# An RWKV-6 attention with a Gelu MLP: later tiles' second product by 20 block products

## The chip, the cores and the metric

The kernel runs on one core of a Trainium2 chip. A time is the device time of one execution in microseconds. Engines are called as in the profile: PE (TensorE's matmuls) and PEld (its weight loads), DVE (VectorE), ACT (ScalarE), POOL (GpSimd), SP (SyncE, which here only issues DMAs). Each works through its own instructions strictly in the order in which they are written.

## What is computed

An attention whose state decays by w at every token, and a two-layer MLP on its output. Batch 4, 8 heads, 768 tokens, head size 48; the attention's output is laid out as x with 3072 tokens of 384; w_in is 384 x 2048, w_out 2048 x 384. All is float32.

```python
for t in range(S):
    cur = einsum('bhd,bhe->bhde', u * k[t], v[t])
    y[t] = einsum('bhd,bhde->bhe', r[t], state + cur)
    state = w[t][..., None] * state + einsum('bhd,bhe->bhde', k[t], v[t])
x = y laid out as (3072, 384)
h = x @ w_in
g = 0.5 * h * (1 + erf(h / sqrt(2)))
out = g @ w_out
```

## The kernel before

**Tiles and stages.** The tokens are cut into eight tiles of T = 384 (NX = 8). For a tile, `attention(x, 0)` gives xT, the transposed input of the MLP, and `mlp(x)` does the MLP. Stage x runs `mlp(x - 1)` together with the end of `attention(x, 0)` and the beginning of `attention(x + 1, 0)`. Stage 0 is attention alone; a last stage, 8, is `mlp(7)` alone.

**The order is written out.** Every part is a Python generator that yields after each small step, and the string `PLAN[x]` says which generator steps next: "." is the MLP's matmuls, "s" and "f" the two attentions (s the one under way, f the following), "l" loads, "x" the eleven sums of x on DVE (`sums_of_x`, L960, tile forms_x), "g" what follows the first product, "w" the sums of the weights, "c" the conversion of the weights. So each engine's queue is fixed by these strings. What holds an instruction back is a semaphore on another engine's work, or a buffer.

**First product (h).** Tile 0 does it plainly (L1093, 128x384 matmuls). Tiles 1 to 7 compute it by 20 block products (`PRODUCTS`, `STEPS`, L1006) for each of two groups q, from sums of blocks of x and w_in. The results are gathered in g, four tiles of 128 x 4 x 384: by copies on ACT (L1025), by accumulating DMAs from POOL ("m", L1052), and by DVE adds from SBUF ("v", L1054) and from PSUM ("+" and "-", L1057). `FOLLOW` lists these merges and the Gelus on ACT (L1067) in one order for each q; a name such as 03 is half 0 of the 384 tokens (192 of them) and group 3 of the 2048 columns of h.

**Second product (out).** It works on blocks of 128 tokens. Tile 0 does its first two blocks plainly, 128x384 (L1181). Tiles 1 to 7 do blocks 0 and 1 by seven products of a 2x2x2 scheme (`product`, L1107, eight matmuls of 128x192 each). The third blocks go in pairs: an even tile (`waits`) keeps its third block apart in `alone`, does two products of it, and the following odd tile (`ends`) does five more on both. The sums of g that the scheme needs (s1, s2, s3) are made by DVE into tiles of their own (`of_g`, L998 to L1002, and L1155 to L1214), those of w_out once, in stage 2 (`w_sums`, `first_sum`). The products alternate between the two PSUM banks that `bank()` hands out in turn.

**PSUM.** Eight banks: from stage 2 on two for `bank()`, two called u0 and u1 (`bank_u`), and two pairs for the attention (`pair`). The attention's last burst of scores (`burst`, L654) uses u0 and u1 in even tiles.

**The attention's order on DVE** that matters here: while the second product of a tile runs, DVE carries the states from chunk to chunk (L792), multiplies u, r and k for the next tile (L457), and then copies two elements of each y bank (`fences`, L830). PE's last matmuls into y (L863) wait for these copies. The six buffers o_sb (`OUTS`) hold saved banks and rows of the output until their DMA has read them.

Of the kernel before, what the change touches and what calls it, by code (L numbers as in the profile page):

```python
# [39 lines left out]
    0: "l.s....llsl.lssslslss.lc.l.slslls...ssss..lcs.s.s.l.ss..ss..sccs.c.s.llpssslw..cs.ffpccxx",  # L40
    1: (
        "scs.ccs..cwsclcs.l.cclcsccssccs.ccc.cswcscccw..swsccls.cccscsc.sscww.lsc.swwcc.ccc.lwllcsl"
        ".fccwcwscc...fccfccws.f.cc.c.w.c.cccfxwcwxcw.c.xx.wcxwcw.fxw.wxx.x.w.fxf.xw.fl."
    ),
    2: (
        "wwws.w.s.wws.w..w..w.gsw..ww.ggw..s..ggwssg.w.ssw.gwgwgg.wslw.ggglww..g.w.s.w..gl..gswgg.s"
        "......wgg.gggg.gglgs.gggggwgs.gs..ssg.lsggs.sgsgwsgw..l.s....s..sssssl..l.lf.sfs.f.ff.lx.w"
        "xxxxxxx.x.xx"
    ),
    3: (  # L50
        "..s....s..s.g.l..g..gsgss....gllgs.ggsg.g..sss.gsgss.s.gs..ggs.g.s.ssg..s.ss.g.s.l.ggsgs.."
        "g.ggggggggssggslgggg.sggg.s....l.sg..sslllss...sslf.ff...xxx.xxxxxx.xx"
    ),
    4: (
        ".s..s.s.sl..s...sgg..s...gg.gg.sg.gl..sgl.ggs...ggg.s.gss.sss...sg.gg.glg...ls.g.sgg.gg.gg"
        "s.sggsgg.g.s.ggs.sg.gsls.g.gssg..sg....ss.sllss.ls..f.ssf.f.f.fx..xx.xxxxlxxfxx"
    ),
    5: (
        ".ls......gls...g.s..s.gl...ggg..gs.sg.ls.gssggsg.gssg.slssss.ls....g..sggsg..ss..ssgg.gsgs"
        "g..g..gggggsgg.ggg.sgg.g.s.sgs.g..sl.l.s.glssfsffs....lfxxxxxxxx..xxx."  # L60
    ),
    6: (
        ".s.ll....sg.s...ss...sg..gssggl.g...gg.sgg..ggss..ggss..s.ss..gs..s.sglggggs...gs.gg..g.g."
        "ggsssgsgsgsg..gg.gg.g...sgggsssg..l...l..s.slsl.s.lf.ss.ff.lff.x..xx.xxxxxfxfxx"
    ),
    7: (
        ".s..s...s...s....gg..g..gs.ggggs...ggg.ssgs.ssgg.s..g.s.gg.s.ssss..s.sgsg..gs.gs..sgg.gggg"
        ".ggggs.g..gsgsg.s.sggg..gg..s.s.sss..ss.xx..xx.x.xxxxxx"
    ),
    8: (  # L70
        "...........g...gg.gg..g.g..ggg.gg..g.g...g.g..gg.g..g...g...gg.gggggg.g.gg.ggg...gggg..g.."
        ".................."
# [50 lines left out]
    "P3", "P12 se", "P17 =cb", "P0 1a00", "P5 =db", "P1 1c03", "P7 1a10", "P8 1b12", "P15 sd+1", "P4 1a11",  # L123
    "P6", "P2 1b02", "P13", "P16 sd+2", "P9 1a13", "P11 sb-", "P10 sa", "P14", "P18", "P19",
)
FOLLOW = (
    (
        "me>00", "md1>11", "me>02", "md2>12", "g00", "mb>03", "ma>03", "+d10", "-c02", "-b13", "G01", "g11",
        "g02", "g10", "g13", "g12", "g03",
    ),  # L130
    (
        "me>00", "md1>11", "me>02", "md2>12", "g00", "vb>03", "va>03", "+d10", "-c02", "-b13", "G01", "g12", "g02",
        "g03", "g13", "g11", "g10",
    ),
# [8 lines left out]
def kernel(  # L143
# [45 lines left out]
    def bank(name="o_ps"):  # L189
        return ps.tile([128, BANK], F32, name=name, tag="mm", bufs=2)  # L190
# [13 lines left out]
    alone = bufs[0][:, ALL:ALL + NF * 128].rearrange("p (f t) -> p f t", f=NF)  # L204
    p1_alone = bufs[0][:, ALL + NF * 128:ALL + NF * 128 + DM // 2]
# [82 lines left out]
    def keep_warm(n, elsewhere=False):  # L288
        if elsewhere:
            t = pair("warm")[:, 0]  # L290
        else:
            t = ps.tile([128, BANK], F32, name="warm", tag="mm", bufs=2)
        for _ in range(n):
            nc.tensor.matmul(t, lhsT=zeros[:, 0:128], rhs=zeros, start=True, stop=True)
# [127 lines left out]
    def attention(x, unit):  # L422
# [183 lines left out]
        def quarters():  # L606
# [28 lines left out]
            for h in QUARTERS:  # L635
                m, r4, t4, s0, s1, s2 = views(h)

                def burst(first, behind, spare=False):

                    d = [bank_u(i) for i in range(2)] if spare else pair("d")  # L640
# [8 lines left out]
                    for n in range(first, behind):  # L649
                        i = n - first  # L650
                        for g in range(2):
                            for p in range(2):
                                o = d[g] if isinstance(d, list) else d[:, g]
                                nc.tensor.matmul(o[half[p], i * 3 * C // 2:(i + 1) * 3 * C // 2],  # L654
                                                 lhsT=kc[half[g], n // NI, n % NI, p],
                                                 rhs=rx[half[g], 2 * n + p], start=not spare or i == 0, stop=True,
                                                 skip_group_check=True)
# [14 lines left out]
                def copy_quarters(first, behind, d):  # L672
                    if isinstance(d, list):
                        for g in range(2):
                            copy_rows(first, behind, d[g][:, 0:(behind - first) * 3 * C // 2].rearrange("p (n x) -> p n x", n=behind - first), g)
                        return
# [14 lines left out]
                whole = last and x % 2 == 0  # L691
                cuts = (0, n_b // 3, 2 * n_b // 3, n_b) if whole else (0, 5, 10, n_b)
                parts_of = list(zip(cuts, cuts[1:]))
                ds = [burst(*parts_of[0])]
                if not whole:
                    yield
                ds.append(burst(*parts_of[1]))
                if whole:
                    ds.append(burst(*parts_of[2], spare=True))
# [3 lines left out]
                if not whole:  # L703
                    ds.append(burst(*parts_of[2]))
                    yield
# [101 lines left out]
        def inside():  # L807

            for b in range(np_):
                if split:  # L810
                    y = [ps.tile([128, BANK], F32, name="y_ps", tag="mm", bufs=2) for _ in range(2)]
                else:
                    y_ps = pair("y_ps")
                    y = [y_ps[:, c] for c in range(2)]
# [82 lines left out]
    HF, HM = NF // 2, DM // 2  # L897
    FG = 4
    sums, s3_sb = [], []

    def w_quarter(b, c, k):
        return w_out_sb[:, b * HF + k * FG:b * HF + (k + 1) * FG, c * HM:(c + 1) * HM]

    def w_sums():

        sums.extend(cv.tile([128, HF, HM], F32, name="t", tag="raw", bufs=AHEAD) for _ in range(3))
        for out_, x, y in ((0, (0, 1), (0, 0)), (1, (1, 1), (0, 1)), (0, (1, 1), 0), (2, (1, 0), 0)):
            for k in range(2):
                o = sums[out_][:, k * FG:(k + 1) * FG]
                nc.vector.tensor_sub(o, w_quarter(*x, k), sums[y][:, k * FG:(k + 1) * FG] if isinstance(y, int) else w_quarter(*y, k))  # L910
                yield

    def first_sum():
        for k in range(2):
            nc.vector.tensor_sub(w_quarter(0, 1, k), w_quarter(0, 1, k), w_quarter(0, 0, k))
            yield

# [3 lines left out]
    s12_of = {}  # L921
    forms_x = const.tile([128, 10, HT], F32, name="forms_x")
    extra = {i: s_home[:, n * 2 * WI:(n + 1) * 2 * WI].rearrange("p (q c) -> p q c", q=HK) for n, i in enumerate((0, 5))}

    def homes():

        more = [cv.tile([128, PIECE], I64, name="s", tag="raw", bufs=AHEAD).bitcast(F32) for _ in range(2)]
        s3_sb.append(more[0][:, 0:HF * 128].rearrange("p (f c) -> p f c", f=HF))
        spare = [cv.tile([128, PIECE], F32, name=name) for name in ("f", "f", "e", "e")]
        for i, name in enumerate(("s1", "s2")):  # L930
            s12_of[name] = [z[:, 0:FG * 128].rearrange("p (f c) -> p f c", f=FG) for z in spare[2 * i:2 * i + 2]]
        for z, at, i in ((more[0], HF * 128, 3), (more[1], 0, 1), (more[1], 2 * WI, 2), (more[1], 4 * WI, 6)):
            extra[i] = z[:, at:at + 2 * WI].rearrange("p (q c) -> p q c", q=HK)
        for n, i in enumerate((4, 7)):
            extra[i] = [z[:, FG * 128:] for z in spare[2 * n:2 * n + 2]]

# [33 lines left out]
    follow_of = {}  # L970

    def follow(x):
        while x in follow_of:
            if next(follow_of[x], follow_of) is follow_of:
                return
            yield

    def mlp(x):

        halves = x > 0
        waits, ends = x % 2 == 0, x % 2 == 1
        gs = {}

        def block(a, b, j):
            return gs[2 * b + j // FG][:, j % FG, a * 128:(a + 1) * 128]

        def store(row0, o_sb, c0=0):
            nc.sync.dma_start(out=out[row0:row0 + 128, c0:c0 + o_sb.shape[1]], in_=o_sb)  # L990

        def of_g(k):

            s1.append(s12_of["s1"][k])
            s2.append(s12_of["s2"][k])
            s3.append(s3_sb[0][:, k * FG:(k + 1) * FG])
            a00, a10, a11 = (gs[g][:, :, a:a + 128] for g, a in ((k, 0), (k, 128), (k + 2, 128)))
            nc.vector.tensor_add(s1[k], a10, a11)  # L998
            yield
            nc.vector.tensor_sub(s2[k], s1[k], a00)  # L1000
            yield
            nc.vector.tensor_sub(s3[k], a00, a10)  # L1002
            yield

        def multiply(o, lhsT, rhs, start=False):
            nc.tensor.matmul(o, lhsT=lhsT, rhs=rhs, start=start, stop=True, skip_group_check=True)  # L1006

        def h_forms():

            for group in range(4):  # L1010
                gs[group] = gp.tile([128, FG, T], F32, name="g")
            banks, saved = {}, {}

            def g_of(q, h):
                a, j = int(h[0]), int(h[1])
# [332 lines left out]
```

## Time and profile before

| what | before |
|---|---|
| median of 3 runs | 593.14 us (592.83 to 593.51) |
| the profiled execution | 591.54 us |
| its span, first to last instruction | 589.4 us |
| mean granted TensorE clock | 0.997 |
| DMAs that accumulate into g | 70, 192 KB each |
| stores of the output | 20 of 192 KB, 8 of 96 KB |

The profile is of one execution. A busy PE is one whose modelled matmuls cover the time. A window is a stretch of the span with each engine's busy time in it. A wait is idle time of an engine just before an instruction, put down to the instruction that released it.

### The profile page before, as it was taken

The page shows a single profiled execution, that of the slowest core. Times are in us where ns is not written, and L with a number is a line of the kernel's source. Part 1 is how long each engine was busy: PE and PEld are TensorE (multiplying, and loading weights), DVE is VectorE, ACT ScalarE, POOL GpSimd, SP SyncE. Part 2 cuts the span into 40 slices and gives each one's busy share as a digit, 9 for nine tenths or more (in the row PEclk, how much of TensorE's full clock was granted, in tenths as well). Part 3 has the DMA queues.
Part 4 walks back from the last instruction along what each step waited for, and adds up shares of the span by engine and source line. Part 5 has one row for each costly group of instructions (what it writes and reads, how often), then busy time and mean ns, then how long its engine had stood idle before and what let it go on. Part 6 is the DMA issues. An engine that isn't in the chain of part 4 may idle for free.

```text
span 589.4 us, 17720 instructions
## 1 busy us (share of the span) xinstructions
PE 561.7 (95%) x7490; PEld 504.0 (86%) x7504; DVE 462.7 (79%) x933; ACT 315.4 (54%) x724; POOL 92.6 (16%) x91
## 2 busy tenths in 40 slices
PE   5789999999999999999999999899999999999997
PEld 3566666699999988897999988898998988999997
DVE  6979979999979986888869997689859997541162
ACT  2358998257542677246652476435771467536600
POOL 3100000034000430023200321004300042005200
PEclk8999999999999999999999999999999999999999
DMA  7649662255152743356322563336533354215500
GB/s 246 206 124 372 209 229 68 68 136 74 23 130 76 146 56 51 113 145 125 42 55 78 149 116 55 82 127 97 70 60 100 86 70 54 41 46 68 68 14 33
DMA packets 70046, 60.59 MB, mean 103 GB/s; under 512 B 32848, under 2 KB 55120, under 8 KB 69968
## 3 DMA queue, kind: packets, MB, share of 16 engines
q1 hardware_dynamic: 50832, 45.62, 25.3%
q0 software_dynamic: 19040, 13.77, 17.9%
q8 instruction: 59, 0.97, 0.7%
q14 instruction: 19, 0.16, 0.1%
q10 hardware_dynamic: 96, 0.07, 0.1%
HBM read 36.24 MB, written 4.72 MB: 69 GB/s over the span
## 4 chain that ended last, share of the span: by engine, by line
PE 39%; DVE 15%; ACT 5%; issue 2%; DMA 1%; SPq 1%; DVEq 0%
PE o_ps L1107 19%; PE h_ps L1006 8%; PE u_ps L1006 5%; DVE rkw L485 3%; PE d L654 3%; DVE kx L451 2%; ACT a_sb L670 2%; DVE rkw L444 2%; DVE st L792 2%; DVE kx L457 2%; PE y_ps L863 2%; DVE forms_x L967 1%; SPq L893 1%; PE kv_ps L777 1%; DMA g<-o_sb 1%
## 5 line engine op out<-in xcount | busy, mean ns | idle before, releaser
L1052 POOL DMA_DIRECT2D g<-o_sb x70 | 84.6, 1264 | 449.5 <-ACT g L1025 413.5
L1006 PE MATMUL h_ps<-forms_x,w_in_sb 128*128 128x192 f32 x280 | 57.3, 332 | 0.0
L1025 ACT COPY g<-h_ps 128x384 f32<-128x384 f32 x84 | 40.2, 481 | 16.6 <-PE h_ps L1006 14.4
L1006 PEld LDWEIGHTS h_ps<-forms_x,w_in_sb 128*128 128x128 f32 x280 | 46.4, 190 | 2.9 <-ACT g L1025 2.1
L1025 ACT COPY o_sb<-u_ps 128x384 f32<-128x384 f32 x42 | 20.2, 481 | 44.6 <-PE u_ps L1006 44.6
L1107 PE MATMUL o_ps<-w_out_sb,g 128*128 128x192 f32 x224 | 39.5, 330 | 4.1 <-ACT g L1067 3.5
L1107 PEld LDWEIGHTS o_ps<-w_out_sb,g 128*128 128x128 f32 x224 | 36.3, 190 | 6.3 <-ACT g L1067 5.3
L670 ACT COPY a_sb<-d 32x256 f32<-32x256 f32 (+8 forms) x90 | 32.6, 363 | 7.6 <-PE d L654 4.2
L1006 PE MATMUL h_ps<-xT,w_in_sb 128*128 128x192 f32 x168 | 35.0, 331 | 1.6 <-DVE g L1057 1.1
L1067 ACT ACTIVATE g<-g 128x384 f32<-128x384 f32 x74 | 35.8, 519 | 0.8 <-DMA g<-o_sb 0.7
L1006 PE MATMUL h_ps<-forms_x,s 128*128 128x192 f32 x168 | 35.8, 336 | 0.3 <-ACT u_ps L1025 0.3
L1093 PE MATMUL h_ps<-xT,w_in_sb 128*128 128x384 f32 x96 | 33.5, 496 | 0.0
L1006 PE MATMUL u_ps<-xT,w_in_sb 128*128 128x192 f32 x168 | 32.7, 331 | 0.8 <-DVE g L1057 0.6
L792 DVE SCALAR_TENSOR_TENSOR st<-st,tot_sb,kv_ps 128x48 f32<-128x48 f32 x160 | 29.1, 256 | 5.3 <-PE kv_ps L777 5.2
L518 PEld LDWEIGHTS d<-rkw 64*64 64x64 f32 x1152 | 19.4, 137 | 14.4 <-issue 9.4
L1107 PE MATMUL o_ps<-w_out_sb,e 128*128 128x192 f32 x176 | 30.9, 328 | 0.5 <-ACT o_sb L1152 0.5
L1107 PE MATMUL o_ps<-t,g 128*128 128x192 f32 x176 | 31.1, 329 | 0.0
L1107 PE MATMUL o_ps<-w_out_sb,f 128*128 128x192 f32 x176 | 31.1, 329 | 0.0
L1107 PE MATMUL o_ps<-t,s 128*128 128x192 f32 x176 | 30.8, 327 | 0.0
L1006 PEld LDWEIGHTS h_ps<-xT,w_in_sb 128*128 128x128 f32 x168 | 28.0, 190 | 3.2 <-DVE g L1057 1.4
L1107 PE MATMUL o_ps<-t,e 128*128 128x192 f32 x176 | 30.5, 326 | 0.0
L1006 PEld LDWEIGHTS h_ps<-forms_x,s 128*128 128x128 f32 x168 | 27.6, 190 | 3.1 <-ACT u_ps L1025 2.3
(177 smaller groups left out, 1268.0 us busy)
## 6 DMA issues: line engine op xcount, KB each, us to landing
rkw<-in_rkw_dram SPq DMA_DIRECT2D x54, 256.0 KB, 3.5
g<-o_sb POOLq DMA_DIRECT2D x70, 192.0 KB, 3.6
raw<-in_w_out_dram SPq DMA_DIRECT2D x8, 768.0 KB, 5.0
v_in<-in_v_dram SPq DMA_DIRECT2D x8, 584.0 KB, 3.9
raw<-in_w_in_dram SPq DMA_DIRECT2D x5, 768.0 KB, 8.2
out_dram<-o_sb SPq DMA_DIRECT2D x20, 192.0 KB, 2.2
rkw<-kx SPq DMA_DIRECT2D x72, 48.0 KB, 2.0
rkw<-in_rkw_dram SPq DMA_DIRECT2D x6, 384.0 KB, 5.1
```

The costliest lines, as they stand in the source:

```text
L444: nc.vector.tensor_reduce(out=fine_sb[:, e, 0:n].rearrange("p a n -> p (a n)"), in_=kx[:, o:o + n * n_m].rearrange("p (m j) -> p m j", j=3 ...
L485: nc.vector.tensor_mul(z, z, by)
L518: nc.tensor.matmul(d[half[p], g, n * width:(n + 1) * width], lhsT=kc[half[g], b, i, p], rhs=right(half[g], b, i, p), start=True, stop=True)
L654: nc.tensor.matmul(o[half[p], i * 3 * C // 2:(i + 1) * 3 * C // 2], lhsT=kc[half[g], n // NI, n % NI, p], rhs=rx[half[g], 2 * n + p], star ...
L670: nc.scalar.copy(out=at[z, g, first:behind, (a + 1) * h:], in_=d[z, :, :, to] if g == slice(None) else d[z, :, to])
L792: nc.vector.scalar_tensor_tensor(out=stq[:, q, c], in0=stq[:, q, c - 1] if c else b4[:, q, NC - 1], scalar=totq[:, q, c:c + 1], in1=kvs[q ...
L1006: nc.tensor.matmul(o, lhsT=lhsT, rhs=rhs, start=start, stop=True, skip_group_check=True)
L1025: nc.scalar.copy(out=o, in_=z)
L1052: nc.gpsimd.dma_start(out=o, in_=saved[q, t], accum_op=ALU.add)
L1067: nc.scalar.activation(out=o, in_=z, func=AF.Gelu, scale=s)
L1093: nc.tensor.matmul(h_ps, lhsT=w_in_sb[:, f // FI, j, f % FI * 128:(f % FI + 1) * 128], rhs=xT[:, j, :], start=(j == 0), stop=(j == NJ - 1))
L1107: nc.tensor.matmul(o, lhsT=lhs(j), rhs=rhs(j), start=start and j == 0, stop=(j == HF - 1), skip_group_check=True)
```

## The change

- Tiles 1 to 7 compute the whole second product by 20 products of a 3x4x2 scheme: three blocks of 128 tokens, four groups of 512 columns of h, two halves of 192 output columns. Each product is four matmuls of 128x192. Pairs of tiles are no longer tied together. `alone` only gives room for sums of w_out.
- The sums of g are made in place, in g itself: 16 adds of 128 x 512 for a tile. A sum may stand only behind the product that reads the earlier content. Ten accumulators share the banks m0, m1, u0 and u1. Some are seeded by a copy of another (S), some are saved (V) and added later (M), and their parts are added to rows of the output by DVE or copied by ACT.
- Tile 0 does all three blocks plainly, the third in a loop of its own.
- In the first product, group q = 0 saves banks c, d and b by ACT ("0sc-", "0sd", "0sb-2") and merges them by accumulating DMAs; these were DVE adds from PSUM. In the last tile all such DMAs become DVE adds.
- `bank()` takes a bank's number. The attention's last burst no longer uses u0 and u1.
- Sums of w_out: 16 in place of 10 blocks, ten of them in stage 1 (stream "y").
- Merges ("v"), Gelus ("g"), sums of g ("o") and copies ("e") are streams of their own, and all of `PLAN` is new.

```diff
+MERGES = (
+    ("me>00", "md1>11", "me>02", "md2>12", "mc>02", "mb>03", "md>10", "mb2>13", "ma>03"),
+    ("me>00", "md1>11", "me>02", "md2>12", "-c02", "vb>03", "va>03", "+d10", "-b13"),
+)
+GELUS = (
+    ("00", "11", "01", "12", "02", "10", "13", "03"),
+    ("00", "11", "12", "02", "03", "10", "13", "01"),
+)
...
+OUT_PRODUCTS = {
+    0: ("A", "11", "w11", False), 1: ("A", "03", "w03", True), 19: ("A", "21", "w00", False),
...
+OUT_BANKS = {
+    "w": "u0", "n6": "m0", "A": "m1", "N4": "u1", "N3": "m0", "n9": "m0", "n11": "m0", "n13": "u0", "D": "m0", "N5": "u0",
+}
+OUT_STEPS = (
+    14, 5, 1, 9, 19, 15, 17, 6, 2, 12, 10, 16, 8, 7, 3, 11, 13, 18, 0, 4,
+)
+OUT_SUMS = (
+    "21+20", "13+03", "20+00", "13+10", "21+00", "00+13", "11+12", "12+02", "N4+01", "22+23", "23+03", "13+22",
+    "22+03", "M9N4", "w-02", "22+02", "n11-02", "M13N4", "11+02", "D+01", "n13+11", "11+01", "11+21", "N4+12",
+    "M11N5", "N5+10", "N5-11", "A-00", "A+10", "D-00",
+)
+OUT_COPIES = (
+    "n6+11", "SAN4", "n6-01", "SAN3", "N3-12", "N3+02", "V9", "n9+00", "V11", "V13", "N4-10", "SDN5",
+)
...
+    def first_mlp():
...
+        for blocks in (0, 1), (2,):
+            o_ps = {i: bank()[:, 0:DM] for i in blocks}
+            for f in range(NF):
+                for i, o in o_ps.items():
+                    nc.tensor.matmul(o, lhsT=gs[f // FG][:, f % FG, i * 128:(i + 1) * 128], rhs=w_out_sb[:, f, :],
+                                     start=(f == 0), stop=(f == NF - 1))
...
+        def sums_of_g():
+            for what in OUT_SUMS:
+                if what[0] == "M":
+                    n, acc = what[1:].split("N")
+                    o = banks["N" + acc]
+                    nc.vector.tensor_add(o, o, saved["n" + n])
+                elif what[0] in "012":
+                    o = g_block(what[0:2])
+                    nc.vector.tensor_add(o, o, g_block(what[3:5]))
...
+            for k in OUT_STEPS:
+                acc, g, w, fresh = OUT_PRODUCTS[k]
+                if fresh:
+                    banks[acc] = psum(acc)
+                z, w = g_block(g), o_block(w)
+                for f in range(FG):
+                    multiply(banks[acc], z[:, f], slice_of(w, f), fresh and f == 0)
+                    if f == FG // 2 - 1:
+                        yield
+                yield
```

## The prediction

> **What bounds the kernel now.** I read the page's first part, then a table of windows cut where one phase of TensorE's work gives way to the next, then the waits of TensorE, then the costliest groups for prices.
>
> ```profile
> span 589.4 us, 17720 instructions
> PE 561.7 (95%) x7490; PEld 504.0 (86%) x7504; DVE 462.7 (79%) x933; ACT 315.4 (54%) x724; POOL 92.6 (16%) x91
> ```
> ```profile
> 254.80:287.60 32.80, 30.83 (x290) 28.20 (x288) 27.85 (x43) 19.89 (x45) 12.03 (x10) 1.00 0.66 127
> 287.60:327.20 39.60, 38.90 (x561) 37.73 (x561) 33.88 (x76) 16.79 (x47) 0.00 (x0) 1.00 0.20 51
> 327.20:361.80 34.60, 33.47 (x385) 30.31 (x384) 31.00 (x48) 22.52 (x55) 12.07 (x10) 1.00 0.65 130
> 361.80:394.50 32.70, 30.62 (x438) 29.55 (x439) 23.94 (x65) 13.68 (x38) 0.00 (x0) 1.00 0.30 78
> 171.00:511.70 340.70, 329.60 (x4149) 310.26 (x4152) 286.35 (x552) 182.09 (x460) 60.33 (x50) 1.00 0.44 90
> ...
> 554.90:589.40 34.50, 31.47 (x192) 31.17 (x192) 13.21 (x27) 4.51 (x12) 0.00 (x0) 1.00 0.06 21
> ```
> The columns are length, busy PE, PEld, DVE, ACT and POOL, the granted clock, the DMA share and GB/s. The first row is the first product of tile 3, the second its second product, the third and fourth the same for tile 4; the fifth is five whole tiles (68.1 us each), the last is the second product of tile 7, with nothing beside it. PE is full in 329.6 of 340.7 us at clock 1.00, so PE bounds the kernel. But DVE has 286.4 of the same 340.7 us, and in the second product of an odd tile it is busy 33.9 of 39.6 us.
>
> ```profile
> PE o_ps L1107 <- ACT g L1067: 3.5, 6, 0.6
> PE y_ps L863 <- DVE fence L830: 2.5, 5, 1.2
> PE h_ps L1006 <- DVE g L1057: 1.1, 1, 1.1
> PE u_ps L1006 <- DVE g L1057: 0.6, 2, 0.5
> ```
> These rows (total us, times, longest) are where PE stops: at the start of each second product for a Gelu, in the attention's output (y) for a DVE copy called fence, and in the first product for DVE's merges, which hold the PSUM banks.
>
> ```profile
> L1181 PE MATMUL o_ps<-w_out_sb,g 128*128 128x384 f32 x64 | 21.2, 489 | 0.0
> L998 DVE TENSOR_TENSOR f<-g 128x512 f32<-128x512 f32 x14 | 9.6, 686 | 6.7 <-ACT g L1067 5.3 <-ACT g L1064 1.3
> L1057 DVE TENSOR_TENSOR g<-g,u_ps 128x384 f32<-128x384 f32 x28 | 14.9, 554 | 10.3 <-PE u_ps L1006 9.9 <-DMA g<-o_sb 0.4
> L1161 DVE TENSOR_TENSOR o_sb<-o_sb,u 128x192 f32<-128x192 f32 x14 | 4.4, 355 | 0.6
> L1052 POOL DMA_DIRECT2D g<-o_sb x70 | 84.6, 1264 | 449.5 <-ACT g L1025 413.5 <-issue 10.6 <-ACT o_sb L1025 8.0
> ```
> Each f32 matmul of the program leaves two records (L1181 is 32 matmuls, x64). A matmul of 384 columns costs 21.2/32 = 0.662 us. In the last window 96 matmuls of 192 columns take 31.47 us, 0.328 us each. The mean ns overlap and aren't used for PE.
>
> **The change, part by part.** Sums are made against the profiled execution's 591.54 us (span 589.4 and 2.14 around it). It lies 1.6 us under the median of 593.14, so 1.6 is added at the end.
>
> *PE work.* Before, second products are 616 matmuls of 192 columns (96 in tiles 1, 3, 5, 7; 72 in 2, 4, 6; 16 for tile 0's third block) and 32 of 384. After, 7 tiles x 20 products x 4 = 560, and 48 of 384. That is -56 x 0.328 = -18.4 and +16 x 0.662 = +10.6: **-7.8 us**. By place: tile 0 +5.3 (+10.6 - 5.3), odd tiles -5.25 each, even ones +2.6. All of it is on PE's path. In the tail (last window) nothing can hide or take it: with DVE busy 13.2 of 34.5 us there, I followed its 20 products at 1.31 us against 30 sums at 0.35 to 0.69 and 12 copies at 0.32. Every sum that a product needs ends before that product starts, the nearest by 0.1 to 0.2 us.
>
> *DVE work.* Sums of 512 columns 88 to 112, +24 x 0.685 = +16.4; PSUM merges of 384 columns 42 to 21, -21 x 0.55 = -11.6; merges from SBUF 14 to 27, all in the last tile, +13 x 0.556 = +7.2; adds of 192 columns 59 to 98, +39 x 0.355 = +13.8; sums of w_out, 10 to 15 of 768 columns at 0.95, some split, +5.1. Together +30.9, so DVE goes from 462.7 to about 494. An inner tile gets +2.7 on average: an even one 5.5 + 2.8 - 1.7 = +6.7, an odd one about 0. Against the windows the second product of a tile then has some 33.7 us of PE (38.9 - 5.25) and some 33.6 of DVE. The cover is nearly gone; what is late next is priced below.
>
> *Waits removed.* The wait of 3.5 us at the start of six second products goes if product 14 finds its Gelus done: it needs only the Gelus of half 11, which stand ahead of five or six others on ACT, where before the first product needed the Gelu that reads the bank PE finishes last (01). Between 0 and -3.5; I take -3.0. In the first product, three PSUM merges of the first half (c, d, b) become copies by ACT and accumulating DMAs, so the banks come free without DVE (1.1 + 0.6 of waits): 0 to -1.7, I take -1.2. The copies are +21 of 0.48 us on ACT; with 44 more of 192 columns (0.32 us), fewer split Gelus and fewer pieces of the attention's scores, ACT gets about +14 us on 315, hidden by its 46% of idle time. If ACT were late, the copies that free a bank would stop PE at once, as 0.5 us does now.
>
> *Waits added.* The fence of y. In the stage of attention 5, DVE must do, from the product's start to the fences: 0.7 us of late merges, 5.2 of attention, 14 sums at 0.60 back to back (8.4), five adds at 0.27 (1.4), the states 3.6, u times k 3.0, fences 0.3, and it waits some 2.3 us on PE for banks: 24.9 us. PE gets to the same place with 15 products (19.5), a burst of d (0.5), kv (1.9) and half of y (1.6): 23.4. So y would wait 1.5 us instead of 0.4. On six tiles the added cost lies between 0 (the planned order holds) and 2 us each, 12; I take +3.5, 0.6 a tile, nearer to the low end because the row nearest to it, the fence's own wait, has 0.5 us a time (2.5 in 5) and 1.2 at the longest. Below zero it can't go: nothing takes DVE work out of that stretch. Behind the fences stand the sums into g that products 11, 0 and 4 read.
>
> *Bank hand-overs.* Banks m0 and u0 are each used by several accumulators (five and three), one after the other, each freed by copies or adds of 0.32 to 0.36 us. At least one product of 1.31 us in another bank stands between every two, so nothing is added beyond the fence's range.
>
> *Stores and loads.* 28 stores become 24. The last is 192 KB (2.2 us) instead of 96 KB (1.6): **+0.6**. SP has no longer queue in front of it.
>
> *First stages.* Tile 0's Gelu is one instruction of 0.49 us instead of 0.373 and 0.272: -2.5 us on ACT, which is 90% busy from 50 to 90 us. Against it the slots of stage 0 stand in a new order and +5.1 us of sums of w_out fall on a DVE that is 97% busy up to 150 us, while PE itself starts tile 1's product 5.3 us later and gives DVE that time. I take 0, between -2 and +5.
>
> Sum: -7.8 - 3.0 - 1.2 + 3.5 + 0.6 = **-7.9**, 583.6; with 1.6, **585.2 us**. All ends favourable: -7.8 - 5.2 + 0.6 - 2 = -14.4, 578.7. All unfavourable: -7.8 + 12 + 0.6 + 5 = +9.8, 603.
>
> **Rivals.**
> *PE's sum alone (0.20).* DVE's late merges bring back the waits at the product's start. For it: DVE is 31.0 of 34.6 us busy in the phase before. Against: halves 11, 10 and 03 are wanted in that order with 1.3 us between. -7.8 + 3.5 + 0.6 = -3.7: 589.4.
>
> *DVE becomes the bound, slower (0.16).* One place: the second product's run of sums up to the fences. Without new waits the change is worth -7.8 - 4.2 + 0.6 = -11.4; over the six tiles with attention beside them it is lost at 1.9 us a tile. At 2.6 us, which needs each of the 14 g sums to take 0.14 us more than I counted, it is +15.6 - 11.4 = +4.2: 597. For it: 33.6 us of DVE against 33.7 of PE, and in order; against: in the even tile's stage before, DVE idles 8.8 of 32.7 us, mostly for single products, and more and shorter products give it finer steps to fit work into.
>
> *Accumulating DMAs late (0.06).* They go from 10 to 13 a tile (70 to 78, the last tile has none) and the second group's merge of half 11 stands on POOL behind ten others. At 1.26 us an issue and 3.6 to land, POOL has 16 us of work in a phase of 33. It decides if that merge, issued some 5 us ahead of product 14, lands more than 1 us late; at 1.9 us on six tiles the time is that of before, 593. The chain of waits has one such DMA on it, 4.04 us at 220.35. The Trainium skill (SBUF — State Buffer, on the port pair that VectorE and GpSimd share) says that a DMA from POOL can stand still while VectorE holds that pair, since its descriptors can't be written. By that rule a busier DVE makes each issue longer; the trace shows a median issue of 1.20 us and a longest of 2.10 with DVE at 90%, so it agrees at most in single cases, and the chance stays small.
>
> **How the numbers follow.** Forecast 0.58 (its own range 579 to 590), PE's sum alone 0.20, late DMAs 0.06, DVE-bound 0.16. Faster than before by over 0.2% (about 1.2 us, what a measurement here can tell) are the first two, 0.77 after a little is taken off for the first stages; the third is the same, 0.06; the last is slower, 0.17. The range goes from the favourable end, 578.5, up to just under the DVE-bound case, 596.
>
> **What would show it.** Right: PE records of second products 1120 of 192 columns and 96 of 384, their last phase about 26 us long from its first matmul to its last; a period of about 67 us a tile; PE's waits on Gelus below 1 us in all; DVE near 494 us. Wrong: a tile period of 69 us or more with PE waiting on the fence, on sums into g or on adds into o_sb (DVE-bound); first matmuls of a second product behind a merge's landing (DMAs); tile 1 starting its first product later than 125 us (first stages).

## The result and the profile after

The changed kernel takes 589.09 us (median of 4 runs, 587.29 to 589.67) against 593.33 us for the kernel before on the same chip: a ratio of 0.9921, 95% interval 0.9895 to 0.9947. It is 4.2 us faster where 8 were forecast. Measured again beside the last experiments it gave 590.84 against 593.49, ratio 0.9958 (0.9938 to 0.9978): a gain of 2.7 us.

The page's first part, of the kernel after:

```profile
span 587.4 us, 17679 instructions
PE 555.5 (95%) x7410; PEld 491.5 (84%) x7424; DVE 490.4 (83%) x997; ACT 330.8 (56%) x733; POOL 103.0 (18%) x99
```

The table of windows, cut as before the change (first and second product of tile 3, the same for tile 4, five whole tiles, the second product of tile 7); the columns are length, PE, PEld, DVE, ACT, POOL, clock, DMA share and GB/s:

```profile
260.20:293.70 33.50, 32.44 (x369) 30.08 (x369) 30.56 (x52) 22.95 (x52) 15.81 (x13) 1.00 0.79 146
293.70:327.90 34.20, 32.45 (x451) 30.58 (x449) 28.77 (x67) 15.63 (x43) 0.00 (x0) 1.00 0.25 64
327.90:362.10 34.20, 32.75 (x369) 30.01 (x368) 30.75 (x53) 23.45 (x53) 15.82 (x13) 1.00 0.76 132
362.10:397.10 35.00, 32.46 (x465) 30.82 (x465) 29.97 (x71) 15.52 (x42) 0.00 (x0) 1.00 0.28 63
176.90:513.60 336.70, 324.75 (x4113) 303.87 (x4112) 298.64 (x586) 193.36 (x470) 79.11 (x65) 1.00 0.51 100
557.70:587.40 29.70, 26.17 (x161) 25.79 (x160) 15.44 (x31) 5.17 (x16) 0.00 (x0) 0.98 0.06 20
```

Five tiles take 336.7 us, 67.3 each (68.1 before); over the three pairs of tiles 1 to 6, from the table below, it is 67.1 each (68.0). The second product of tile 3 went from 39.6 to 34.2 us, that of tile 4 from 32.7 to 35.0, the tail from 34.5 to 29.7. PE now stands still 12.0 of these 336.7 us (11.1 before). The largest waits of PE from tile 1 on:

```profile
PE y_ps L908 <- DVE fence L875: 3.4, 4, 1.6
PE h_ps L1040 <- DVE o_sb L1167: 3.3, 4, 1.1
PE d L708 <- DVE kx L684: 1.6, 4, 0.6
PE u_ps L1040 <- ACT u_ps L1084: 1.2, 2, 0.9
```

The Gelu waits at the start of the second products (3.5 us) are gone. The second row is new: the first product's third step waits for VectorE to add bank m0, the bank of the accumulator D, into a row of the output.

Tile by tile, a table worked out from the first matmul of each phase in PE's timelines (us; "start" is the first matmul of tile 0's first product, "T1" to "T7" the length of each tile from its first matmul to the next tile's, T7 to PE's last matmul):

```
                 start  start->T1    T1     T2     T3     T4     T5     T6     T7
before           45.97    73.31   70.56  64.96  72.40  66.40  70.08  63.80  58.92
after            49.20    79.09   64.65  67.24  67.68  69.25  65.50  68.11  53.15
difference       +3.23    +5.78   -5.91  +2.28  -4.72  +2.85  -4.58  +4.31  -5.77
PE work             0      +5.3   -5.25   +2.6  -5.25   +2.6  -5.25   +2.6  -5.25
```

From tile 1's first matmul on the change gains 11.5 us (467.1 to 455.6), of PE's 13.1. In tile 0 it pays 5.8. What is left over is stage 0, 3.2 us later in this pair of executions. So two questions: does the change cost those 3.2 us, and how near is VectorE to setting the time?

### The profile page after: what moved, and what is told of

It is laid out like the page before. It is cut to its first block, busy times and chain, and to the rows that moved or that the text cites. A ratio compares the mean times of both kernels' runs of the same rounds, so it can differ in the third digit from the quotient of the medians.

```text
span 587.4 us, 17679 instructions
## 1 busy us (share of the span) xinstructions
PE 555.5 (95%) x7410; PEld 491.5 (84%) x7424; DVE 490.4 (83%) x997; ACT 330.8 (56%) x733; POOL 103.0 (18%) x99
## 5 line engine op out<-in xcount | busy, mean ns | idle before, releaser
L1164 DVE TENSOR_TENSOR g<-g 128x512 f32<-128x512 f32 x112 | 74.4, 686 | 21.8 <-PE o_ps L1040 19.2
L1084 ACT COPY o_sb<-u_ps 128x384 f32<-128x384 f32 (+1 forms) x56 | 25.6, 457 | 61.0 <-PE u_ps L1040 57.9
L1040 PE MATMUL o_ps<-w_out_sb,g 128*128 128x192 f32 x280 | 50.1, 326 | 0.0
L1133 ACT ACTIVATE g<-g 128x384 f32<-128x384 f32 x98 | 47.0, 521 | 0.7 <-DMA g<-o_sb 0.4
L724 ACT COPY a_sb<-d 32x320 f32<-32x320 f32 (+5 forms) x108 | 39.1, 362 | 3.2 <-DVE a_sb L782 1.0
L1040 PEld LDWEIGHTS o_ps<-t,g 128*128 128x128 f32 x224 | 36.8, 190 | 0.3
L708 PE MATMUL d<-kx,rkw 64*64 64x96 f32 x1152 | 30.7, 247 | 1.8 <-DVE kx L684 1.6
L1040 PE MATMUL u_ps<-w_out_sb,g 128*128 128x192 f32 x168 | 31.1, 333 | 1.2 <-ACT u_ps L1084 1.2
L708 PEld LDWEIGHTS d<-kx,rkw 64*64 64x64 f32 x1152 | 25.3, 133 | 7.4 <-issue 3.6
L1059 PE MATMUL o_ps<-w_out_sb,g 128*128 128x384 f32 x96 | 31.4, 488 | 0.0
```

The source lines that it names most:

```text
L708: nc.tensor.matmul(d[half[p], g, i * 3 * C // 2:(i + 1) * 3 * C // 2], lhsT=kc[half[g], n // NI, n % NI, p], rhs=rx[half[g], 2 * n + p], s ...
L724: nc.scalar.copy(out=at[z, g, first:behind, (a + 1) * h:], in_=d[z, :, :, to] if g == slice(None) else d[z, :, to])
L1059: nc.tensor.matmul(o, lhsT=gs[f // FG][:, f % FG, i * 128:(i + 1) * 128], rhs=w_out_sb[:, f, :], start=(f == 0), stop=(f == NF - 1))
L1084: nc.scalar.copy(out=o, in_=z)
L1133: nc.scalar.activation(out=o, in_=z, func=AF.Gelu, scale=MINUS.get(h, 1.0))
L1164: nc.vector.tensor_add(o, o, g_block(what[3:5]))
```

## The experiments

Each ratio below is to the kernel before on the same chip. The changed kernel itself is at 0.9921 and 0.9958.

**Stage 0 in its old order, and the new order in the kernel before.**

```diff
-     0: ".xll.s...lcsl.ssslsslsls.l.slll..scls.ls.cpc.ss..csss..sscsl.sc...lsc.ssss.ls.l...sf.wfxpf",
+     0: "l.s....llsl.lssslslss.lc.l.slslls...ssss..lcs.s.s.l.ss..ss..sccs.c.s.llpssslw..cs.ffpccxxf",
```

> The changed kernel with stage 0 in its old order (one step of the next attention put behind it, so that the counts of the later stages agree); nothing else differs. Theory A, the new slot order of stage 0 cost 3.7 us: tile 0's first product starts at about 46 us instead of 49.2, tile 1's at about 124.5 instead of 128.3, and the time is about 585.4 us, 3 to 4 below the changed kernel's 589.1. Rival B, the delay comes from the added sums of w_out and what stage 1 holds, not from stage 0: 589 us, with the first product of tile 0 at 49 or the gain given back before tile 1's product starts.

> The kernel before with the changed kernel's order of stage 0 (without its third step of the next attention). Theory A: the order alone costs what it cost in the changed kernel, so tile 0's first product starts at about 49 us instead of 46 and the time is 596 to 597 us, against 593.3. Rival B: the stages behind take the delay up, since their work has other waits to hide it in: 593 to 594 us.

The first measured 588.4 us, ratio 0.9888 (0.9848 to 0.9927); the second 595.86, ratio 1.0027 (0.9999 to 1.0055), 1.6 us and anything from nothing to 3.3, so neither theory A nor rival B is excluded for the kernel before. Tile 0's first matmul stands at 45.43 us with the old order and at 47.41 with the new. But in the changed kernel the 3.8 us that stage 0 won are given back before tile 1, which starts at 127.63 instead of 128.29. Some 1.7 us of that are the clock's and not the order's: in this execution the granted clock fell to 0.50 between 71 and 75 us, inside tile 0 (an estimate, half of that time). So the profiles leave the old order some 2.4 us at best, where theory A said 3 to 4, and point to rival B. The times don't settle it: the interval holds the changed kernel's first ratio, 0.9921, and lies below the interval of its second, 0.9938 to 0.9978.

**The changed kernel once more, as it is.**

> The changed kernel once more, as it is, beside the next two. If stage 0 differs from execution to execution by as much as the 3.2 us between the two first profiles (tile 0's first matmul at 45.97 and 49.20 us; the same order gave 45.2 to 51.0 in the runs since), it starts anywhere in that range, and the rest of the time, from tile 1's first matmul to the end, stays at 455 to 456 us. If the order of stage 0 sets it, tile 0 starts within 0.5 us of 49.2.

590.84 us, ratio 0.9958. This execution reached tile 0 at 50.73 us and then took 454.67 us from tile 1's first matmul to the end (455.58 in the first profile). So what comes after tile 1's start repeats within 1 us, and stage 0 doesn't. Windows of this run around the end of stage 0, the granted clock being the third number from the right:

```profile
40.00:43.00 3.00, 1.39 (x39) 1.31 (x41) 2.89 (x7) 0.33 (x1) 0.00 (x0) 0.96 0.21 50
43.00:46.00 3.00, 3.00 (x101) 2.85 (x101) 2.84 (x7) 2.96 (x7) 0.00 (x0) 0.50 0.89 292
46.00:49.00 3.00, 2.50 (x44) 1.36 (x45) 0.57 (x2) 2.54 (x3) 0.00 (x0) 0.50 1.04 396
49.00:52.00 3.00, 3.00 (x69) 2.45 (x64) 1.14 (x1) 0.00 (x0) 0.00 (x0) 0.50 1.06 403
```

PE was busy 1.39 of 3 us, from 40 to 43, and then ran at half its clock for 9 us. The Trainium skill (TensorE: Matmul & The Clock Gate, Part 1) says that the array's clock is halved after an idle window of some 3.4 us, and that the window runs free of the program, so that the same kernel meets it differently each time. The trace agrees with the halving and with the chance in it, 0.50 here and 1.00 in the same stretch of the first profile; the window was not idle here, but busy to 46%. Over all profiled executions of this study with the new order tile 0's first matmul lies between 45.2 and 51.0 us (ten, mean 48.5), with the old order between 45.0 and 46.0 (four, mean 45.5). So the later start is the new order's, 3.0 us in the mean. The clock is only part of it: five of the ten have no fall of the clock between 20 us and tile 0, and they start at 46.9 to 49.2. The new order leaves PE emptier (3.18 and 3.17 of 5 us from 25 to 35 us, before 4.56 and 4.57).

**The fence issued ahead of the next tile's u times k.**

```diff
-            ... "s..lsel.l.ooosfes..o..folo.e" ...
+            ... "s..lsel.l.ooossfe..o..folo.e" ...
```

The "s" behind the first "f" in stages 3 to 6 (it issues y and its fence, "f" u times k) is moved ahead of it; in the diff, the piece of stage 3's order.

> The changed kernel with the fence of y issued ahead of the next attention's u times k (four instructions, 3.0 us on VectorE) in stages 3 to 6. Theory A, the fence is late because that work stands ahead of it: the waits of y for the fence in stage 5 (2.4 us of the 3.4) go, and the time falls by 1.5 to 2.4 us, to about 587. Rival B, VectorE is behind by a sum and not by an order: what leaves the fence comes back as waits for sums, forms of x or kx within the same tile, and the time stays at 589.

590.54 us, ratio 0.9949 (0.9922 to 0.9976): no gain. Theory A said the fence would come earlier, and it does. Here is VectorE in the changed kernel from the states on, and then in this one from the second fence on:

```profile
380.60 2.54 DVE L837 SCALAR_TENSOR_TENSOR st<-st,tot_sb,kv_ps 128x48 f32<-128x48 f32 x14 [0.29 <-PE kv_ps L822]
383.05 0.36 DVE L1161 TENSOR_TENSOR u_ps<-u_ps,o_sb 128x192 f32<-128x192 f32 x1
383.32 0.78 DVE L837 SCALAR_TENSOR_TENSOR st<-st,tot_sb,kv_ps 128x48 f32<-128x48 f32 x4
384.02 0.68 DVE L1164 TENSOR_TENSOR g<-g 128x512 f32<-128x512 f32 x1
384.62 3.03 DVE L512 SCALAR_TENSOR_TENSOR kx<-rkw,u_sb,rkw 128x384 f32<-128x384 f32 x4
387.49 0.21 DVE L875 COPY fence<-y_ps 128x2 f32<-128x2 f32 x2
387.61 0.35 DVE L1167 TENSOR_TENSOR o_sb<-o_sb,o_ps 128x192 f32<-128x192 f32 x1
```
```profile
385.48 0.16 DVE L875 COPY fence<-y_ps 128x2 f32<-128x2 f32 x1 [0.56 <-PE y_ps L863]
385.85 3.07 DVE L512 SCALAR_TENSOR_TENSOR kx<-rkw,u_sb,rkw 128x384 f32<-128x384 f32 x4 [0.21 <-issue]
388.75 0.36 DVE L1167 TENSOR_TENSOR o_sb<-o_sb,o_ps 128x192 f32<-128x192 f32 x1
```

And PE behind it, in the changed kernel and then in the one with the early fence:

```profile
387.72 1.64 PE L908 MATMUL y_ps<-rkw,st 64*64 64x64 f32 x96 [1.57 <-DVE fence L875]
389.30 1.57 PE L1040 MATMUL o_ps<-t,g 128*128 128x192 f32 x8
```
```profile
386.83 1.63 PE L908 MATMUL y_ps<-rkw,st 64*64 64x64 f32 x96
389.16 1.57 PE L1040 MATMUL o_ps<-t,g 128*128 128x192 f32 x8 [0.70 <-DVE o_sb L1167]
```

PE reaches its last matmuls into y 0.9 us earlier (386.83 instead of 387.72), and waits at the next product instead, for the add that u times k now stands ahead of: that product starts at 389.16, in the changed kernel at 389.30. Rival B's outcome, in its own place.

**Two of the sums of g by an accumulating DMA.**

```diff
-                    nc.vector.tensor_add(o, o, g_block(what[3:5]))
+                    if what in ("12+02", "22+02") and x < NX - 1:
+                        nc.gpsimd.dma_start(out=o, in_=g_block(what[3:5]), accum_op=ALU.add)
+                    else:
+                        nc.vector.tensor_add(o, o, g_block(what[3:5]))
```

> The changed kernel with two of the 16 sums of g of tiles 1 to 6 (block 12 plus 02, block 22 plus 02) done by an accumulating DMA issued on POOL, which is idle in that phase; their sums are first read 7 to 15 us later. VectorE gets 1.24 us a tile less, POOL 12 issues more. Theory A (moving the fence gave nothing because VectorE is behind by a sum): the waits of y for the fence (3.4 us) and for kx (1.6) shrink by half or more and the time falls by 2 to 3 us, to about 586.5. Rival B: the DMA, longer than a merge's 4.0 us since it moves 256 KB in pieces of 512 bytes, is late for product 18 or 3, and PE waits for it: 589 or more.

591.98 us, ratio 0.9996 (0.9972 to 1.0021): no faster than the changed kernel, by the ratios rather slower. The DMAs land in 5.0 us and no product waits for one, so rival B's reason falls; but theory A falls too. The waits for the fence are still 3.3 us. The trace of the changed kernel shown above says why: after its last pause, at kv (380.60, 0.29 us idle), VectorE works without a gap to the fence, 6.9 us. Ahead of that point it had pauses of 0.98, 0.20, 0.58 and 0.94 us, all but the second waiting for PE. The two sums stood between these pauses, and without them the pauses are longer: 0.43 and 1.19 us in place of the first, 0.86 and 0.26 in place of the 0.29 at kv. The profile of this kernel is of its longest execution (596.18 us), in which the clock fell twice before tile 1. Its stretch from tile 1 on is 3.4 us longer: 1.8 us are two waits behind a PSUM merge (L1120) that VectorE does later than in the changed kernel, 0.4 more stand behind the row in m0. Why VectorE comes to those merges later, and the rest, is not settled.

**All sums of g left out.**

```diff
-                    nc.vector.tensor_add(o, o, g_block(what[3:5]))
+                    pass
```

> The changed kernel without its 16 sums of 512 columns of g per tile (112 in all, 69 us of VectorE); everything else is issued as before. It leaves part of the second product's computation out (its values are not the reference's), so its time is only that of the rest. Theory A, VectorE is near its limit but PE sets the time: only the waits of PE that hang on VectorE's lateness go, the fence's 3.4 us, most of kx's 1.6 and part of the 3.3 behind the sum into o_sb: 4 to 7 us, 582 to 585. Rival B, VectorE bounds the inner tiles: the period falls by more than 2 us a tile and the time below 575.

585.9 us, ratio 0.9883 (0.9855 to 0.9912). From tile 1 on it takes 451.67 us, 3.9 less than with the sums, for 69 us less of VectorE. So 65 of these 69 us are hidden: VectorE doesn't bound the second products.

**Merges of the first product back on VectorE.**

```diff
-    "P6 0sc-", "P2 cb02", ... "P14 0sd", "P18 0sb-2", "P19",
+    "P6", "P2 cb02 0-c02", ... "P14 0+d10", "P18 0-b13", "P19",
-    (... "mc>02", "mb>03", "md>10", "mb2>13", "ma>03"),
+    (... "1-c02", "mb>03", "1+d10", "1-b13", "ma>03"),
```

A 0 or 1 in front of a name means that it is done for that group alone. So in group 0 the three merges are issued right behind the products, and the three new names in the list do nothing there.

> The changed kernel with the three merges of the first half (c, d and b into g) done by VectorE from PSUM again, instead of by a copy of ScalarE and an accumulating DMA: 21 sums of 0.55 us more on VectorE (11.6 us), 21 copies less on ScalarE, 18 DMAs less on POOL. Theory A, what I priced at 1.2 us was the waits for the banks: 1 to 3 us slower than the changed kernel, 590 to 592. Rival B, VectorE has no cover left: its 1.65 us a tile come out whole in the period, 8 to 11 us slower. Rival C: no change, the copies only moved idle time.

599.84 us, ratio 1.0108 (1.0075 to 1.0140): slower than the kernel before, and 9 to 11 us slower than the changed kernel. Rival B: from tile 1 on the kernel takes 12.3 us longer, for 9.9 us of VectorE in the six tiles whose merges moved (tile 7 has no DMAs in either kernel). Some 1.7 of the 12.3 us are the clock's: behind a wait of PE of 2.0 us it stood at 0.50 from 353.6 to 357 us, in tile 4 (an estimate, half of that time). Some 10.6 are left. The waits of PE, those on VectorE and ScalarE that grew:

```profile
PE d L708 <- DVE kx L684: 4.2, 4, 1.7
...
PE u_ps L1040 <- DVE g L1120: 2.9, 2, 1.8
...
PE h_ps L1040 <- DVE g L1120: 2.3, 1, 2.3
PE h_ps L1040 <- ACT u_ps L1084: 2.0, 1, 2.0
```

Tile 7 keeps its 53.2 us; tiles 1 to 6 lose 2.2, 2.0, 0.0, 4.4 (with the clock's 1.7), 1.4 and 2.3. The order was not remade for this kernel, so this is what the merges cost in the changed kernel's order, not in the best one; whether VectorE's time or the place of the merges in its queue costs it, this run doesn't tell.

**Tile 0's third block left out, and then VectorE's work beside it lightened.**

```diff
-        for blocks in (0, 1), (2,):
+        for blocks in ((0, 1),):
```

> The changed kernel without the third block of tile 0's second product (16 matmuls of 384 columns, 10.6 us); it leaves those 128 rows of the output out, so its time is that of the rest. Theory A, PE's work alone sets when tile 1 starts: the stretch from tile 0's first matmul to tile 1's falls from 79.1 to 68.5 us, and the time by 10 to 10.6 us, to about 579. Rival B, VectorE (98 to 100% busy between 100 and 130 us) has the sums of w_out and of w_in to do there, and the third block only hides them: the stretch falls by no more than 5 to 7 us and tile 1 starts with waits for VectorE.

```diff
+                if first == 0:
+                    nc.scalar.copy(out=po, in_=pa)
```

> As the kernel without tile 0's third block, and besides that the first ten sums of w_out (10 us of VectorE in stage 1) are plain copies by ScalarE, which is idle there; the 128 rows are left out and the second products use wrong weights, so its time is that of the rest. Theory A, VectorE bounds the stretch from tile 0's first matmul to tile 2's, so that taking 10.6 us from PE alone gave nothing: now the stretch falls from 145 to 136 to 138 us, and the time by 7 to 9 us. Rival B, another thing (ScalarE's Gelus, the loads) holds it: 143 to 145 us.

Without the third block the time is 589.44 us, ratio 0.9938 (0.9903 to 0.9972): nothing gained for 10.6 us of PE. Tile 1 does start 8.75 us earlier after tile 0, but takes 74.82 instead of 64.65 us; the stretch from tile 0's first matmul to tile 2's is 145.2 us, with the block 143.7. PE's waits in between:

```profile
PE h_ps L1040 <- ACT g L1084: 4.6, 1, 4.6
PE u_ps L1040 <- DVE s_home L1020: 2.5, 1, 2.5
```

The second is a sum of w_in that VectorE comes to only then; VectorE works without a pause from 100 to 140 us. The other is a copy on ScalarE that stands behind an attention copy waiting for VectorE. Behind the wait of 4.6 us the granted clock, too, stood near 0.50 from 134 to 137.7 us, some 1.7 us of PE's time (an estimate, from the share of clock missing). So rival B: in stage 1 VectorE is full and so, with the block, is PE, and tile 0's third block is the cover for the sums. The second kernel took 586.17 us, ratio 0.9871 (0.9828 to 0.9914), its stretch 141.7 us, between the two expectations. It proves less than it was made for: the ten copies stood in ScalarE's queue ahead of those that free the banks, and PE waited 5.0 us for one of them, at the end of which the clock fell, to 0.50 from 126.5 to 133 us. What VectorE alone would give back there stays open.

**D's products before A's.**

```diff
+INNER_STEPS = OUT_STEPS[:-2] + (4, 0)
+INNER_SUMS = OUT_SUMS[:-3] + ("D-00", "A-00", "A+10")
...
-            for what in OUT_SUMS:
+            for what in OUT_SUMS if x == NX - 1 else INNER_SUMS:
...
-            for k in OUT_STEPS:
+            for k in OUT_STEPS if x == NX - 1 else INNER_STEPS:
```

This holds for tiles 1 to 6. In the orders of stages 2 to 7 one "o" near the end moves ahead of an "x" or two besides, so that the add of D stands straight behind its product.

> The changed kernel with the last two block products of tiles 1 to 6 exchanged (D's before A's), so that bank m0, which the next first product needs at its third step, is read out one product earlier; the sum into row block 0 stands straight behind its product. Theory A: the waits of the third step for the sum into o_sb (3.3 us in four) fall below 0.7 us, and the time by 2 to 3 us, to about 586.5. Rival B: the wait moves to bank m1, needed 0.66 us later, or to the forms of x in front of the same step: 588.5 to 589.5.

> The changed kernel with the old order of stage 0 and D's products before A's. From tile 1's first matmul to the end: 453.3 us, as D before A gave, 2.3 less than the changed kernel. Theory A, the order of stage 0 costs about 1.6 us (the middle of what the kernel before lost by it): time 2.3 + 1.6 = 4 us below the changed kernel of the same chip. Rival B, the order costs nothing and only single executions differ: 2.3 us below it.

586.12 us, ratio 0.9873 (0.9824 to 0.9921); with the old stage 0 besides, 586.05, ratio 0.9890 (0.9856 to 0.9924). Of the kernels that compute everything these are the fastest; the second is clearly faster than the changed kernel measured beside it (0.9938 to 0.9978), the first by its trace. From tile 1 on they take 453.25 and 453.75 us, 2.3 and 1.8 less than the changed kernel. The wait, in the first of them:

```profile
PE h_ps L1042 <- DVE o_sb L1169: 0.3, 1, 0.3
```

It was 3.3 us. The waits for kx grew meanwhile, from 1.6 us to 2.7. Between these two kernels, whose clock is steady from 20 us on, the old order of stage 0 brings nothing, as rival B says: it gives tile 0 its first matmul at 45.54 us and tile 1 its own at 126.15, where the first has 47.04 and 126.23.

**One merge more by DMA.**

```diff
-    ... "P6 0sc-" ...   "me>00", "md1>11", "me>02", "md2>12", "-c02", "vb>03" ...   "00", "11", "12", "02", "03", "10", "13", "01"
+    ... "P6 sc-" ...    "me>00", "md1>11", "me>02", "md2>12", "mc>02", "vb>03" ...  "00", "11", "12", "03", "10", "13", "01", "02"
```

> The kernel of old stage 0 and D first, and besides that the merge of c into half 02 of the second group goes by a copy and an accumulating DMA in tiles 1 to 6, as in the first group, with that half's Gelu last: VectorE 0.55 us a tile less, ScalarE 0.48 more, POOL one issue more. Theory A: a merge on VectorE costs in the first product what moving 21 of them back showed (10.7 us, 0.5 each), so 6 less give 2 to 3 us more than the kernel it is made from. Rival B: those 10.7 us came from an order that was not made for them; VectorE has room, and the DMA's landing holds ScalarE's last Gelu: 0 to 2 us slower than the kernel it is made from.

585.19 us, ratio 0.9874 (0.9840 to 0.9909), beside 0.9890 for the kernel that it is made from: no difference that can be told. Tiles 1 to 6 together take 2.0 us less (398.9 and 400.9), the lower end of theory A, and tile 7 takes 54.11 instead of 52.90: there the new order of the Gelus takes halves 03 and 10 ahead of their last merges, so that its values are not the reference's. Of the 2.0 us, 1.1 are tile 1's, behind a tile 0 in which the clock stood at 0.50 for some 3 us. The direction is theory A's, for 3.3 us of VectorE; that it is worth having isn't shown.

## Why the prediction was right, and where not

Right: the sign, the range (578.5 to 596, a wide one), and what carries it, PE's sum. Too good by 3.9 us: about half of the gain forecast came, and by the second measurement a third. The time lies on the figure of the rival "PE's sum alone" (589.4) by chance, since what that rival rests on, the Gelu waits coming back, did not happen.

*PE work, -7.8.* The tiles' differences follow it, odd tiles -4.6 to -5.9 (-5.25 said), even ones +2.3 to +4.3 (+2.6). Tile 0 has its 96 records of 384 columns (31.4 us), and the tail 26.2 us of PE, as walked through.

*Waits removed.* The Gelu waits went whole, 3.5 (3.0 taken). The bank waits behind VectorE's merges, 1.7, shrank to 0.3 behind a copy. As a term that is right, but it hid the weight of that part: with the three merges on VectorE the changed kernel, in its order, is slower than the one before. The prediction put the rival "VectorE becomes the bound" into the second product, with a break-even of 1.9 us a tile; in this order it is the first product's merges, 1.65 us a tile, that cost more than the whole gain. In the second, 10 us a tile of sums cost 0.6 (3.9 in seven tiles).

*Fence, +3.5.* It was mis-sized: the waits of y went from 3.0 to 3.9 us, +0.9. In the stage of attention 5 the walk came out (1.5 said, 1.6 measured), but it was set against the wrong wait: "instead of 0.4" is what y waited in tiles 1 and 3, while in this stage, tile 4's second product, the kernel before already waited 1.2 us (the longest of its row, 1.2). So the change added 0.3 there and not 1.1. The other three waits of the row have 0.2 to 0.8 us, and some stages none. To take 0.6 a tile on top of what was there was the error.

*Bank hand-overs, nothing.* This step failed: "at least one product of 1.31 us in another bank stands between every two" looks at the second product alone. The last bank of a tile, m0, is handed to the next tile's first product, whose third step asks for it 1.5 us after PE's last matmul into it, while VectorE has the next attention's work in front of the add. 3.3 us in four tiles; reading D out first took it away.

*First stages, nothing between -2 and +5.* The profile pair shows +3.2 in stage 0 and +0.5 behind it, tile 1 starting at 128.3 where 125 was named as the sign of an error. The 3.2 is about what the new order costs tile 0's start in the mean (3.0), but most of it doesn't reach tile 1. With a steady clock from 20 us on tile 1 starts at 126.2 to 128.3 us in the changed kernel and its variants (five executions, one with the old order of stage 0; mean 126.9), and at 119.3 and 120.4 in the kernel before (the second with the new order). That is 7.0 us later in the mean, where PE's sum has 5.3. So the first stages cost some 1.7 us, an estimate from few executions, and more where the clock falls in stage 0 (tile 1 at 131.7 when measured again). The reason given for nothing, that PE's third block gives VectorE the time for the added sums, fits what the kernel without that block shows; where the 1.7 us come from was not taken apart.

*The rest.* VectorE got 27.7 us (30.9 said), ScalarE 15.4 (14), the period is 67.3 (67), the last store and what follows it +0.5 (+0.6). A wait of 1.2 us for ScalarE's copy that seeds an accumulator, and 1.6 for kx, were not in the sum. From tile 1 on the rows named here add up: PE -13.1, Gelus -3.5, banks -1.4, fence +0.9, m0 +3.3, kx +1.6 and the seed +1.2 make -11.0, and -11.5 was measured. Luck had a part in it: the fence priced 2.6 us too high stood against 6.1 us of waits that were not priced.

The profile pair alone differs by 2.4 us (591.54 and 589.16). The execution before lay 1.6 under its median, and was corrected for.

*Accumulating DMAs late.* The records of the issue on POOL have 1.50 us in the mean instead of 1.26, the longest 2.73 instead of 2.10, the landing 4.0 instead of 3.6; PE waited for none. The first row is all of them, the second four issues in a row:

```profile
L1115 POOL DMA_DIRECT2D g<-o_sb x78 | 95.0, 1504 | 378.5 <-ACT g L1084 312.5 <-DVE tot_sb L532 41.6 <-DMA g<-o_sb 19.2
```
```profile
274.31 4.91 POOL L1115 DMA_DIRECT2D g<-o_sb  x4 [1.65 <-DMA g<-o_sb]
```

The issue itself did not get longer. POOL is busy 95.0 us for 78 issues, 1.22 each, and before it was 84.6 us for 70, 1.21 each. The four in a row take 4.91 us, 1.23 each, but each one's record begins before the one ahead has ended, so the records have 1.2, 1.7, 2.2 and 2.7 us. The longer mean is that of more issues in a row, and so were the 2.10 us of the prediction, the last of three. That VectorE is busy 490.4 us in place of 462.7 doesn't show in it. The Trainium skill (SBUF — State Buffer, on the port pair that VectorE and GpSimd share) ties the stall to VectorE's two-port modes and reports that its probe did not see it beside `tensor_tensor`. The sums and adds that the change gives VectorE are of that kind, so the page's rule does not make each issue longer here, as the prediction took it to, and the trace agrees with the page.

## What to carry to other kernels

Ask of each wait on a busy engine what that engine does between its own last pause and the instruction waited for. Only that stretch can shorten the wait: work taken from ahead of the pause only lengthens the pause, and work moved from ahead of the instruction to behind it makes the next consumer wait.

Follow every buffer across the seam between phases: the accumulator that is read out last decides when the next phase gets its bank. And when a part of a change is priced by the waits it removes, ask also what would come back without it, since an engine's time can be free in one phase (65 of 69 us hidden) and cost in full in the next (9.9 us put back, in an order not made for them, cost some 10.6).

## What the runs showed of the hardware

The granted clock fell to 0.50 at gaps of PE: at waits of 4.6 and 5.0 us (the two kernels without tile 0's third block), at one of 2.0 us (the merges on VectorE), and in stage 0 of the changed kernel after 3 us in which PE was busy 46%. It stayed there for 3 to 9 us, with PE busy or nearly so. Between 20 us and tile 0 five of the ten executions with the new order of stage 0 had such a fall, and the four with the old order had none (two of these had one inside tile 0). One and the same order of stage 0 ended anywhere between 45.2 and 51.0 us, a spread larger than the whole effect of the change; the clock is a part of that spread, and the rest is open. From 140 us to PE's last matmul the clock was at 1.00 in every run but for those 3 us of the merges on VectorE, and the changed kernel's time from tile 1 on repeated within 1 us.

An accumulating DMA of 192 KB kept POOL busy for 1.21 to 1.22 us. Issued one behind the other, their records overlap, and the mean of the records, 1.50 us, is not the cost of one.
